# A fused attention and gated MLP kernel: the first batch's heads keep keys, queries and two value blocks in SBUF between two passes

## The chip, the core and the metric

The kernel runs on one core of one Trainium2 chip. The metric is device time in microseconds (us), the median of the runs shown. TensorE (PE) multiplies matrices, VectorE (DVE), ScalarE (ACT) and GpSimd (POOL) work element by element, SyncE (SP) issues the loads and stores. SBUF is the memory on the chip, PSUM the banks that PE writes.

## What is computed

Causal attention with a bias from a running sum, for 8 batches of 8 heads (576 tokens, head size 64), and behind it a gated MLP whose gate mixes tokens:

```python
scores = scale * np.matmul(q, k.transpose(0, 1, 3, 2))
cum = np.cumsum(np.maximum(s, 0.0), axis=-1)
bias = -(cum[:, :, :, None] - cum[:, :, None, :])
scores = np.where(causal, -1000000000.0, scores + np.minimum(bias, 0.0))
attn = softmax(scores); x = heads of attn @ v, side by side
h = gelu(x @ w_in); u, v = halves of h
v_n = (v - mean) / sqrt(var + 1e-06) * g_ln
v_s = np.einsum('ts,bsd->btd', w_sg, v_n) + b_sg[None, :, None]
out = x + (u * v_s) @ w_out
```

## The kernel before

Every batch's eight heads go through scores (PE, into PSUM), a masked reduction that also finds the maximum (DVE; CUSTOM_DVE in the profile, ISA in the order lists), exp with its sum (ACT), a reciprocal (DVE) and a scaling (POOL, ACT or DVE), PE transposes ("turned" below, with `ident`), copies from PSUM (`pT`), and the product with the values, two heads at a time. The MLP of a batch (`ffn`) has v units (values and layer norm), u units, s units (the gate, first product `ws` x `vn`) and o units (`wo`); matrices are split into a hi and a lo part (`split`), so that three products in fp32r stand for one in fp32. All matmuls of the MLP and of heads 8 to 63 work on such parts.

The first batch is special, since nothing has been split when the kernel starts. Its eight heads (`SPL = 8`) use unsplit fp32 and go through in two passes: `scores_a`/`context_a` for the first 320 tokens (`CA`), `scores_b`/`context_b` for the other 256 (`CB`) against all keys. In the first pass the bias comes from a product of `sel` with the running sums (`cc`, tile xs), in the second from two rows of running sums (`cum`) that a small load puts below the keys. Meanwhile the weights arrive as 64-bit floats (`pair<-in_w_in`), are put together on ACT and DVE (`psm<-pair`, `gt<-pair`) and split into `wi` and `wo`; `w_sg` is split into `ws` by `w_sg_part`. Before the two-pass work is through, FFN units have little to multiply; 49 matmuls on a constant (`WARM = 9`, `FILL = 40`, `psm<-wt`) fill PE's time.

The places of the first batch: `load_a` (line 702 on) brings queries and keys of the first pass into `kqs[0..2]` (heads 0 to 2, over the rings k1, q1, k2), or into `arena` (heads 3 to 7, over `wo`). `load_va` brings value blocks for the first pass into `early`, over `ws`. `load_b` brings the 256 queries and all 576 keys of the second pass anew (832 columns) into `kqs[3]`, `kqs[4]` (over vn) or into `arena` where a head of the first pass was; `load_vb` brings five value blocks anew. Upper halves of these tiles are set to 0 or 1 by memsets. Scores have three buffers while the first eight heads run: p_66, p_68 and e_71 (`pslot`), so heads 0, 3, 6 share one, as do 1, 4, 7 and 2, 5.

The order on all engines is written by a planner (`Plan`). Every step is put at a time by `POS`, the planner lists operations with their dependences and walks them by priority; `SHIFT`, a table of one offset for each operation, moves priorities. `pick` chooses the engine of a step from the letters in `ENG` and `ALT` (s ACT, g POOL, v DVE). The planner's order is fixed when the kernel is built; on the chip every engine works through its own list in order. `w_sg_part` may begin when head 5's second pass is turned (its assert), since `ws` lies over `early`.

## Time and profile before

| | |
|---|---|
| median of 3 runs | 738.69 us (736.52 to 740.17) |
| the profiled execution | 737.75 us, span 736.0 us |
| busy: PE, DVE, ACT, POOL | 726.3, 483.4, 482.8, 526.0 us |
| granted TensorE clock over the span | 0.999 |
| DMA: moved, mean rate | 88.35 MB, 120 GB/s |

The span runs from the first instruction to the last; the profiled execution's own time has 1.75 us around it. Busy times add what an engine's instructions cover. All lines of the profile carry one line number, that of the planner's `issue` (L441; L446 in the changed kernel), so work is told apart by its tiles: `p<-pss,mask` is a score piece leaving PSUM, `wi<-gt,wi` the lo part of w_in, and so on. An entry in square brackets says how long the engine had been idle and what ended that.

### The profile page before, as it was taken

Reading aid. Unit: us, or ns where it says so; the run is one execution under the profiler, and the core shown is the slowest. Engines: PE = TensorE matmul, PEld = TensorE weight load, DVE = VectorE, ACT = ScalarE, POOL = GpSimd, SP = SyncE. Lnnn points to the kernel's source line nnn. Section 1 sums busy time; section 2 is a strip of 40 time slices with the busy share of each in tenths; the row PEclk is TensorE's granted clock in tenths of the full one; section 3 lists DMA queues with packets and bytes.
Section 4 is the critical chain, followed back from the end, with each engine's and each line's share of the span. In section 5 each row is a group of like instructions: output and inputs, shape, how many; then the busy total and the mean of one; then the engine's idle time right before and its main releaser. Section 6 shows DMA issues by size and latency. Waiting matters only on the chain.

```text
span 736.0 us, 16276 instructions
## 1 busy us (share of the span) xinstructions
PE 726.3 (99%) x5337; PEld 640.8 (87%) x5337; DVE 483.4 (66%) x1524; ACT 482.8 (66%) x1306; POOL 526.0 (71%) x941
## 2 busy tenths in 40 slices
...
GB/s 210 252 234 102 199 125 121 169 141 149 128 135 133 130 115 104 124 110 124 147 86 119 123 125 127 106 92 144 132 108 119 95 135 114 61 9 34 47 9 64
DMA packets 59272, 88.35 MB, mean 120 GB/s; under 512 B 16306, under 2 KB 33972, under 8 KB 59188
## 3 DMA queue, kind: packets, MB, share of 16 engines
...
## 4 chain that ended last, share of the span: by engine, by line
PE 91%; DVE 3%; DMA 2%; POOL 2%; ACT 1%; issue 1%; SPq 1%; ACTq 0%; DVEq 0%; POOLq 0%
PE psm L441 54%; PE psp L441 21%; PE pss L441 15%; DMA pair<-in_w_in 1%; DVE p L441 1%; SPq L441 1%; DVE psm L441 1%; POOL p L441 0%; DMA raw<-in_kq 0%; POOL wi L441 0%; POOL rt L441 0%; ACT p L441 0%; DVE gt L441 0%; DVE vt L441 0%; DVE u L441 0%
## 5 line engine op out<-in xcount | busy, mean ns | idle before, releaser
L441 POOL TENSOR_SCALAR p<-p,rs 64x64 f32<-64x64 f32 (+4 forms) x396 | 177.8, 458 | 55.9 <-DVE rs L441 37.8
L441 ACT ACTIVATE p<-p,mn 64x64 f32<-64x64 f32 (+4 forms) x310 | 172.5, 558 | 57.4 <-DVE mn L441 55.7
L441 DVE CUSTOM_DVE_ANT_0 p<-pss,mask 128x448 f32<-128x448 f32 (+4 forms) x304 | 121.0, 425 | 37.0 <-PE pss L441 27.7
L441 PE MATMUL psm<-gt,wo 128*128 128x288 f32 x720 | 125.0, 299 | 0.0
L441 PE MATMUL pss<-k,q 128*128 128x288 f32 (+9 forms) x672 | 122.2, 297 | 0.2
L441 PE MATMUL psm<-xs,wi 128*128 128x288 f32 x720 | 119.3, 300 | 0.0
L441 PE MATMUL psm<-ws,vn 128*128 128x288 f32 x708 | 114.1, 297 | 0.0
L441 PEld LDWEIGHTS pss<-k,q 66*128 66x128 f32 (+3 forms) x672 | 102.2, 180 | 9.3 <-DVE mn L441 0.5
L441 POOL TENSOR_TENSOR k<-raw,k 128x576 fp32r<-128x576 f32 x54 | 77.3, 1431 | 44.8 <-ACT k L441 41.1
L441 PE MATMUL psm<-wi,xs 128*128 128x512 f32 (+1 forms) x380 | 106.6, 401 | 1.0 <-DVE gt L441 1.0
L441 PEld LDWEIGHTS psm<-gt,wo 128*128 128x128 f32 x720 | 105.3, 188 | 1.7
L441 PEld LDWEIGHTS psm<-xs,wi 128*128 128x128 f32 x720 | 102.6, 188 | 2.4 <-issue 0.4
L441 PEld LDWEIGHTS psm<-ws,vn 128*128 128x128 f32 x708 | 100.2, 188 | 0.9 <-DVE vt L441 0.3
L441 PE MATMUL psp<-pT,vf 128*64 128x64 f32 (+3 forms) x752 | 90.1, 387 | 0.0
L441 PEld LDWEIGHTS psp<-pT,vf 128*64 128x64 f32 x752 | 46.9, 137 | 43.9 <-issue 32.1
L441 PEld LDWEIGHTS psm<-wi,xs 128*128 128x128 f32 (+1 forms) x380 | 66.3, 184 | 13.2 <-DVE gt L441 1.2
L441 ACT COPY pT<-psp 128x512 f32<-128x512 f32 x130 | 72.0, 581 | 8.7 <-PE psp L441 8.1
L441 PE MATMUL psp<-ident,p 128*128 128x128 f32 x744 | 72.3, 247 | 0.3 <-POOL p L441 0.3
L441 PEld LDWEIGHTS psp<-ident,p 128*128 128x128 f32 x744 | 69.7, 140 | 3.0 <-POOL p L441 0.5
L441 DVE SCALAR_TENSOR_TENSOR u<-u,psm 128x288 f32<-128x288 f32 x120 | 52.7, 445 | 18.6 <-ACT u L441 18.2
L441 POOL TENSOR_TENSOR gt<-u,gt 128x288 fp32r<-128x288 f32 (+1 forms) x62 | 49.6, 804 | 18.7 <-ACT gt L441 18.2
L441 ACT ACTIVATION_READ_ACCUMULATOR p<-p,mn 128x1 f32 (+1 forms) x310 | 58.5, 189 | 0.0
...
## 6 DMA issues: line engine op xcount, KB each, us to landing
q<-k SPq DMA_DIRECT2D x168, 144.0 KB
...
```

The costliest lines, as they stand in the source:

```text
L441: fn(*args, **kw)
```

## The change

The eight heads of the first batch get a place each (`own`) that holds first- and second-pass data side by side: heads 0 to 2 in `kqs[0..2]`, 3 to 5 in `arena`, 1152 columns each (`TW`: 320 queries, 320 keys, then 256 keys, 256 queries); heads 6 and 7 get 1024 columns each in `kqs[3]`, where the second-pass queries take the place of the first-pass ones. `load_a` writes the first 640 columns. `load_b` loads only the 256 new keys and 256 new queries (one load of 512 columns, or two of 256 for heads 6 and 7), and the rows of running sums. `load_vb` loads three value blocks; blocks 0 and 1 are read in the second pass from where `load_va` put them (`sums_of`). So `early` is needed until the last pair of the second pass, and `w_sg_part` now begins after all four pairs (assert, and `POS["ws"]` from 7.0 to 8.2). `kqs[4]` goes. Memsets change with the places. `norm`'s first step can be put on another engine (`ra`), but its letter is ACT's as before. `SHIFT` (table cut here) and `ALT` are new throughout.

```diff
-A0 = 3
-AG = ((0,), (1,), (2,), (3, 4), (5, 6, 7))
+AG = ((0,), (1,), (2,), (3, 4), (5,), (6, 7))
+TW = 2 * S
 VG = ((0, 1), (2, 3), (4, 5, 6, 7))
 U2 = 7
-ENG = dict(kh="s", kl="g", xh="g", xl="g", gh="s", gl="g", wh="s", wl="g", wsh="s", wsl="gggv", n="g", vl="g", ev="s",
+ENG = dict(ra="s", kh="s", kl="g", xh="g", xl="g", gh="s", gl="g", wh="s", wl="g", wsh="s", wsl="gggv", n="g", vl="g", ev="s",
            ev1="v", xv="s", xz="v", xw="v", th="s", rt="g", na="sgg", nb="g", ea="ss", eb="s", eb1="vv", xa="sgss", xal="g",
            xva="s", xvb="v")
 ALT = {
...
-    "wh": "sssvvggssggg",
...
-    "nb": "gggsvsggggssvggsggv",
-    "eb1": "ssvsvsvv",
...
+    "wh": "ssssgsssgssg",
...
+    "nb": "vggsgsggsgssggsgssggsggs",
+    "eb1": "vvvvvvvv",
...
-           wu=(2.267, 6.052), ws=(7.001, 10.088), wo=(8.179, 8.76), f0=10.787, a=(0.058, 0.283), la=-0.795, va=-0.44,
+           wu=(2.267, 6.052), ws=(8.2, 10.7), wo=(8.179, 8.76), f0=10.787, a=(0.058, 0.283), la=-0.795, va=-0.44,
...
             p0, f0 = divmod(ap.offset, pat[0][0])
             f1 = f0 + sum(st * (c - 1) for st, c in pat[1:]) + 1
             out = []
+            w = (slot[1] - slot[0]) // 4
             for i, x in enumerate(slot):
-                lo, hi = max(f0, i * S), min(f1, i * S + S)
+                lo, hi = max(f0, i * w), min(f1, i * w + w)
                 if lo < hi:
-                    out.append((x, p0, p0 + pat[0][1], lo - i * S, hi - i * S))
+                    out.append((x, p0, p0 + pat[0][1], lo - i * w, hi - i * w))
             return out
         assert name in self.live.get(slot, (name,)), name
         ps = pat[0][0] or 1
...
                 prio = self.backward(lat, [t + o.busy for t, o in zip(self.start, ops)])
         if SHIFT:
             shift = np.frombuffer(zlib.decompress(base64.b85decode(SHIFT)), np.int16)
-            res = self.forward(lat, [p + 200.0 * float(x) for p, x in zip(prio, shift)])
+            res = self.forward(lat, [p + 100.0 * float(x) for p, x in zip(prio, shift)])
         return res
 
     def walk(self, left, follow, place, prio, begin=0.0, hold=False):
...
         d["raw"] = att.tile([P, S], F32, name="raw", tag="raw", bufs=1)
         nc.sync.dma_start(out=d["raw"], in_=kq[h, 0:2 * D])
 
+    def own(h):
+        return (kqs[h], 0, TW) if h < 3 else (arena, (h - 3) * TW, TW) if h < 6 else (kqs[3], (h - 6) * 1024, 1024)
+
     def load_a(i):
         g = AG[i]
-        if g[0] < A0:
-            t = kqs[g[0]][:, 0:2 * CA]
+        t, o, w = own(g[0])
+        for j, h in enumerate(g):
+            heads.setdefault((h, 0), {}).update(q=t[:, o + w * j:o + w * j + CA], k=t[:, o + w * j + CA:o + w * j + 2 * CA])
+        dst, src = t[0:D, o:o + w * len(g)], ka[:, g[0] * 2 * CA:(g[-1] + 1) * 2 * CA]
+        if len(g) > 1:
+            dst = dst.rearrange("p (h w) -> p h w", w=w)[:, :, 0:2 * CA]
+            src = src.rearrange("p (h w) -> p h w", w=2 * CA)
         else:
-            t = arena[:, (g[0] - A0) * 2 * CA:(g[-1] + 1 - A0) * 2 * CA]
-        for j, h in enumerate(g):
-            o = 2 * CA * j
-            heads[h, 0] = {"q": t[:, o:o + CA], "k": t[:, o + CA:o + 2 * CA]}
-        nc.sync.dma_start(out=t[0:D], in_=ka[:, g[0] * 2 * CA:(g[-1] + 1) * 2 * CA])
+            dst = dst[:, 0:2 * CA]
+        nc.sync.dma_start(out=dst, in_=src)
 
     def load_va(i):
         g = VG[i]
         t = early[0][:, 3 * S + g[0] * 4 * D:3 * S + (g[-1] + 1) * 4 * D]
         nc.sync.dma_start(out=t, in_=va[:, g[0] * 4 * D:(g[-1] + 1) * 4 * D])
         for j, h in enumerate(g):
-            heads[h, 0]["v"] = t[:, j * 4 * D:(j + 1) * 4 * D].rearrange("p (a d) -> p a d", d=D)
+            heads.setdefault((h, 0), {})["v"] = t[:, j * 4 * D:(j + 1) * 4 * D].rearrange("p (a d) -> p a d", d=D)
 
     def load_b(h):
+        assert (scores_a, h) in done
         d = heads[h, 1] = {}
-        w = CB + S
-        n = (3, 4, "t", 0, 1, 2, 3, 4)[h]
-        if h > 5:
-            assert (scores_b, h - 6) in done
-        if h > 1 and h < 6:
-            t = arena[:, AW:AW + w] if n == "t" else arena[:, n * w:n * w + w]
-            if n != "t":
-                assert all((scores_a, i) in done for i in range(A0, SPL))
-                nc.gpsimd.memset(t[D:P, 0:CB], 1.0)
+        t, o, _ = own(h)
+        m = o + 2 * CA
+        d["k"] = t[:, o + CA:o + CA + S]
+        if h < 6:
+            d["q"] = t[:, m + CB:m + 2 * CB]
+            nc.sync.dma_start(out=t[0:D, m:m + 2 * CB], in_=kb[h])
         else:
-            t = kqs[n][:, CA - CB:CA + S]
-        d["q"], d["k"] = t[:, 0:CB], t[:, CB:w]
-        nc.sync.dma_start(out=t[0:D], in_=kb[h])
-        nc.sync.dma_start(out=t[D:66, CB:w], in_=cum[:, h, :])
+            d["q"] = t[:, o:o + CB]
+            nc.sync.dma_start(out=t[0:D, m:m + CB], in_=kb[h][:, 0:CB])
+            nc.sync.dma_start(out=t[0:D, o:o + CB], in_=kb[h][:, CB:2 * CB])
+        nc.sync.dma_start(out=t[D:66, o + CA:o + CA + S], in_=cum[:, h, :])
 
     def load_vb(h):
         d = heads[h, 1]
-        d["v"] = att.tile([P, 5, D], F32, name="vf", tag="vf")
-        nc.sync.dma_start(out=d["v"], in_=vp[h, :, 0:5])
+        d["v"] = att.tile([P, 3, D], F32, name="vf", tag="vf")
+        nc.sync.dma_start(out=d["v"], in_=vp[h, :, 2:5])
 
     def load_v(h):
         d = heads.setdefault(h, {})
...
         nc.tensor.matmul(wm, wt.broadcast_to([P, P]), wt.broadcast_to([P, 512]), start=True, stop=True)
     nc.after = 850.0
     wo = const.tile([P, NC, 2, DM], F32R, name="wo")
-    AW = (SPL - A0) * 2 * CA
     arena = nc0.alloc_sbuf_tensor_at(f"arena_{next(Ring.serial)}", [P, NC * 2 * DM], F32, offset=Ring.top - NC * 2 * DM * 4).ap()
     nc.home[arena.tensor.name] = nc.home[wo.tensor.name]
     nc.live[nc.home[wo.tensor.name]].add(arena.tensor.name)
-    nc.vector.memset(arena[D:P, 0:2 * 2 * CA], 0.0)
-    nc.gpsimd.memset(arena[D:P, 2 * 2 * CA:AW], 0.0)
-    nc.gpsimd.memset(arena[D:P, AW:AW + CB], 1.0)
-    nc.gpsimd.memset(arena[D:P, AW + CB:AW + CB + S], 0.0)
     kqs = []
-    for i in range(5):
+    for i in range(4):
         if i < 3:
             r = pools[("k1", "q1", "k2")[i]]
-            t = nc0.alloc_sbuf_tensor_at(f"kq_{i}", [P, CA + S], F32, offset=r.at[0]).ap()
-            slots = nc.home[t.tensor.name] = tuple(r.at[0:2])
-            for x in slots:
-                nc.live[x] = {t.tensor.name}
+            t = nc0.alloc_sbuf_tensor_at(f"kq_{i}", [P, TW], F32, offset=r.at[0]).ap()
+            slots = tuple(r.at[0:2])
         else:
-            t = pools["vn"]([P, CA + S], F32, "kq", i - 1)
-        nc.gpsimd.memset(t[D:P, 0:CA], 1.0)
-        nc.gpsimd.memset(t[D:P, CA:2 * CA if i < 3 else CA + S], 0.0)
+            t = nc0.alloc_sbuf_tensor_at(f"kq_{i}", [P, 2048], F32, offset=pools["vn"].at[2]).ap()
+            slots = tuple(pools["vn"].at[2:4])
+        nc.home[t.tensor.name] = slots
+        for x in slots:
+            nc.live[x] = {t.tensor.name}
         kqs.append(t)
+
+    def plain(e, t, a, b):
+        e.memset(t[D:P, a:b], 0.0)
+
+    for i in range(3):
+        plain(nc.gpsimd, kqs[i], 0, 2 * CA)
+    plain(nc.vector, arena, 0, 2 * CA)
+    plain(nc.gpsimd, arena, TW, TW + 2 * CA)
+    plain(nc.gpsimd, arena, 2 * TW, 2 * TW + 2 * CA)
+    for i in range(2):
+        nc.gpsimd.memset(kqs[3][D:P, 1024 * i:1024 * i + CA], 1.0)
+        plain(nc.gpsimd, kqs[3], 1024 * i + CA, 1024 * i + CA + S)
+    for i in range(3):
+        for t, o in ((kqs[i], 0), (arena, i * TW)):
+            nc.gpsimd.memset(t[D:P, o + 2 * CA + CB:o + TW], 1.0)
+            plain(nc.gpsimd, t, o + 2 * CA, o + 2 * CA + CB)
     cf = moe.tile([P, S], F32, name="cf", tag="xs", bufs=4)
     nc.scalar.activation(out=st[0:BH], in_=st[0:BH], func=AF.Relu, scale=8.0)
     nc.vector.tensor_tensor_scan(out=cf[0:BH], data0=wt.bitcast(F32)[0:BH].broadcast_to([BH, S]), data1=st[0:BH],
...
                 yield 1
 
     def w_sg_part():
-        assert all((context_b, h) in done for h in range(SPL) if pslot(h) == 2)
+        assert all((xsplit, c) in done for c in range(NC))
         for j in range(NT):
             for f in range(2):
                 fs = slice(f * CH, f * CH + CH)
...
             yield 1
 
     def w_out_part():
-        assert all((scores_b, h) in done for h in range(2, 6))
+        assert all((scores_b, h) in done for h in range(3, 6))
         for c in range(NC):
             part(wide, w_out[c * P:(c + 1) * P], wo[:, c, 0, :], wo[:, c, 1, :])
             yield 1
...
 
     def norm(h, its, rs):
         c = slice(min(its), max(its) + 1)
-        nc.scalar.activation(out=rs[:, c], in_=sums[pslot(h)][:, c], func=AF.Copy, bias=1e-9)
+        e = pick("ra")
+        if e is nc.scalar:
+            e.activation(out=rs[:, c], in_=sums[pslot(h)][:, c], func=AF.Copy, bias=1e-9)
+        else:
+            e.tensor_scalar(out=rs[:, c], in0=sums[pslot(h)][:, c], scalar1=1e-9, scalar2=None, op0=ALU.add)
         nc.vector.reciprocal(out=rs[:, c], in_=rs[:, c])
         for it in its:
             r, w = ITR[it], ITW[it]
...
         with nc.group():
             for o0, o1, jt, c0, kw in parts:
                 for side, i in enumerate(pair):
-                    nc.tensor.matmul(x[D * side:D * side + D, o0:o1], heads[i, half]["v"][:, jt, :],
+                    v = heads[i, 0]["v"][:, jt, :] if jt < 2 or not half else heads[i, 1]["v"][:, jt - 2, :]
+                    nc.tensor.matmul(x[D * side:D * side + D, o0:o1], v,
                                      pts[i % NPT][:, c + c0:c + c0 + o1 - o0], **{"start": False, "stop": False, **kw})
 
     def context_a(h):
...
     va = np.concatenate([v[0:SPL, 0:CA], z, z, v[0:SPL, 0:D]], axis=1)
     return {
         "ka": np.concatenate([qt[:, :, 0:CA], kt[:, :, 0:CA]], axis=2).transpose(1, 0, 2).reshape(D, SPL * 2 * CA),
-        "kb": np.concatenate([qt[:, :, CA:S], kt], axis=2),
+        "kb": np.concatenate([kt[:, :, CA:S], qt[:, :, CA:S]], axis=2),
         "va": va.reshape(SPL, 4, P, D).transpose(2, 0, 1, 3).reshape(P, SPL * 4 * D),
         "kq": kq,
         "vp": v6.reshape(BH, 6, P, D).transpose(0, 2, 1, 3),
```

SP's list from its start, before (kq_80 to kq_82 are heads 0 to 2, pair is w_in, e_71 the value blocks, kq_83 and kq_84 the later `kqs`):

```order
L441 DMA xs_76<-in_s_t 64x576
L441 DMA kq_80<-in_ka 64x640
L441 DMA kq_82<-in_ka 64x640
L441 DMA pair_105<-in_w_in 128x1024
L441 DMA kq_81<-in_ka 64x640
L441 DMA e_71<-in_va 128x512
L441 DMA pair_121<-in_w_in 128x1024
L441 DMA arena_79<-in_ka 64x1280
L441 DMA pair_112<-in_w_in 128x1024
L441 DMA e_71<-in_va 128x512
L441 DMA kq_83<-in_kb 64x832
L441 DMA arena_79<-in_ka 64x1920
```

and after the change:

```order
L446 DMA xs_76<-in_s_t 64x576
L446 DMA pair_104<-in_w_in 128x1024
L446 DMA kq_80<-in_ka 64x640
L446 DMA pair_111<-in_w_in 128x1024
L446 DMA arena_79<-in_ka 64x640
L446 DMA kq_81<-in_ka 64x640
L446 DMA kq_82<-in_ka 64x640
L446 DMA kq_83<-in_ka 64x2x640
L446 DMA arena_79<-in_ka 64x2x640
L446 DMA e_71<-in_va 128x512
L446 DMA pair_120<-in_w_in 128x1024
```

A w_in tile has moved ahead of the first head, and all first-half loads ahead of the value blocks, the third w_in tile and the second-half loads.

POOL's list around the scalings of head 2 (e_71), before:

```order
L441 TENSOR_TENSOR wi_99<-gt_113,wi_99 128x512
L441 MEMSET e_71 128x64
L441 TENSOR_SCALAR e_71<-e_71,rs_110 64x64
L441 TENSOR_SCALAR e_71<-e_71,rs_110 128x320
L441 TENSOR_SCALAR e_71<-e_71,rs_110 64x64
L441 TENSOR_TENSOR wi_99<-gt_106,wi_99 128x512
L441 TENSOR_SCALAR xs_125<-xr_115 128x320
L441 MEMSET arena_79 64x256
```

and after:

```order
L446 TENSOR_TENSOR wi_98<-gt_105,wi_98 128x512
L446 MEMSET kq_82 64x256 x2
L446 MEMSET kq_80 64x256
L446 MEMSET e_71 128x64
L446 MEMSET kq_83 64x576
L446 TENSOR_SCALAR p_68<-p_68,rs_107 128x128
L446 TENSOR_SCALAR p_68<-p_68,rs_107 128x320
L446 MEMSET kq_80 64x256
L446 MEMSET kq_83 64x320
L446 MEMSET kq_83 64x576
L446 TENSOR_SCALAR e_71<-e_71,rs_109 128x320
L446 TENSOR_SCALAR e_71<-e_71,rs_109 64x64 x2
```

The lo part of a w_in tile that stood just ahead of head 2 is now ahead of head 1 too, and the memsets have come between.

POOL's list where the lo parts of w_sg begin, before (p_66 with rs_187 is head 6's second pass):

```order
L441 TENSOR_SCALAR p_66<-p_66,rs_187 128x512
L441 TENSOR_SCALAR p_66<-p_66,rs_187 64x64
L441 TENSOR_TENSOR xs_131<-xr_120,xs_131 128x256
L441 TENSOR_TENSOR ws_70<-u_113_185,ws_70 128x288
L441 TENSOR_TENSOR ws_70<-u_121_193,ws_70 128x288
```

and after (p_66 with rs_202 is head 8):

```order
L446 TENSOR_SCALAR p_66<-p_66,rs_202 128x448
L446 TENSOR_TENSOR ws_70<-u_125_198,ws_70 128x288
L446 TENSOR_SCALAR p_66<-p_66,rs_202 64x64
L446 TENSOR_TENSOR ws_70<-u_132_205,ws_70 128x288
L446 TENSOR_TENSOR k_151_224<-raw_219,k_150_223 128x576
L446 TENSOR_TENSOR ws_70<-u_137_210,ws_70 128x288
L446 TENSOR_TENSOR xs_138<-xr_134,xs_138 128x256
L446 TENSOR_TENSOR wo_78<-gt_200,wo_78 128x512
```

They have moved from behind head 6's second pass to behind most of head 8's scalings.

## Rows read from the trace of the kernel before

**Rows 1.** The page, busy time, share of the span and instructions of two engines.

```profile
PE 726.3 (99%) x5337; PEld 640.8 (87%) x5337; DVE 483.4 (66%) x1524; ACT 482.8 (66%) x1306; POOL 526.0 (71%) x941
```

**Rows 2.** Busy time in four stretches: us, PE, PEld, DVE, ACT, POOL, PEclk, DMA share, GB/s.

```profile
10.00:30.00 20.00, 19.26 (x141) 16.34 (x141) 14.88 (x62) 16.26 (x61) 10.08 (x22) 1.00 1.04 262
30.00:90.00 60.00, 57.37 (x418) 45.07 (x415) 57.17 (x168) 54.15 (x148) 44.60 (x71) 1.00 0.68 179
90.00:106.00 16.00, 15.69 (x107) 12.33 (x106) 13.73 (x44) 12.95 (x38) 14.35 (x32) 1.00 0.51 124
106.00:720.00 614.00, 613.86 (x4561) 548.65 (x4562) 387.24 (x1227) 394.41 (x1054) 445.56 (x791) 1.00 0.41 109
```

**Rows 3.** DMA issues of the first 60 us: out<-in, count, KB each.

```profile
vf<-in_vp SPq DMA_DIRECT2D x6, 160.0 KB
...
kq<-in_kb SPq DMA_DIRECT2D x4, 208.0 KB
arena<-in_kb SPq DMA_DIRECT2D x4, 208.0 KB
...
kq<-in_ka SPq DMA_DIRECT2D x3, 160.0 KB
```

**Rows 4.** The chain that ended last and PE's timeline, 5 to 10 us.

```profile
5.39 10.55 DMA pair<-in_w_in
...
5.26 1.03 PE L441 MATMUL pss<-kq 128*128 128x320 f32 x4
...
8.94 1.10 PE L441 MATMUL pss<-kq 128*128 128x320 f32 x4 [1.78 <-DMA kq<-in_ka]
9.75 0.56 PE L441 MATMUL pss<-xs,sel 128*128 128x192 f32 x2
```

**Rows 5.** Timelines of POOL, PE and DVE, 14 to 27 us (start, us, engine, work).

```profile
14.66 0.37 POOL L441 TENSOR_SCALAR p<-p,rs 128x128 f32<-128x128 f32 x1 [5.24 <-DVE rs L441]
...
20.14 1.27 POOL L441 TENSOR_TENSOR wi<-gt,wi 128x512 fp32r<-128x512 f32 x1 [0.93 <-ACT rs L441]
...
24.68 0.31 POOL L441 MEMSET arena<- 64x256 f32 x1
...
25.06 0.51 PE L441 MATMUL psp<-ident,e 128*128 128x128 f32 x4 [0.50 <-POOL arena L441]
...
26.02 0.36 DVE L441 CUSTOM_DVE_ANT_0 e<-pss,mask 128x192 f32<-128x192 f32 x1
```

**Rows 6.** DVE's timeline, 14 to 25 us: the entries ahead of which it waited.

```profile
16.68 0.70 DVE L441 TENSOR_SCALAR psm<-psm 128x512 int32<-128x512 int32 x1 [1.28 <-ACT psm L441]
...
19.52 0.36 DVE L441 CUSTOM_DVE_ANT_0 p<-pss,mask 128x192 f32<-128x192 f32 x1 [0.68 <-PE psp L441]
...
22.96 0.49 DVE L441 COPY xr<-psp 128x320 f32<-128x320 f32 x1 [1.61 <-PE psp L441]
...
24.11 0.17 DVE L441 RECIPROCAL rs<-rs 128x3 f32<-128x3 f32 x1 [0.65 <-ACT rs L441]
```

**Rows 7.** DVE's groups by shape, 30 to 100 us: count, busy us, mean ns.

```profile
L441 DVE SCALAR_TENSOR_TENSOR gt<-pair,psm 128x512 int32<-128x512 int32 x9 | 6.1, 674 | 0.0
L441 DVE COPY pT<-psp 128x512 f32<-128x512 f32 x7 | 4.7, 674 | 0.0
```

**Rows 8.** The tile ws: duration in ns min/median/max, first and last start.

```profile
L441 POOL TENSOR_TENSOR ws<-u,ws x6: 805/808/814, 74.4 to 87.0; 128x288 fp32r<-128x288 f32 x6
```

**Rows 9.** Timelines of PE and POOL, 57 to 104 us.

```profile
57.03 1.02 PE L441 MATMUL pss<-arena 128*128 128x448 f32 x2 [1.62 <-DVE mn L441]
...
81.18 2.29 PE L441 MATMUL psp<-pT,vf 128*64 128x256 f32 x20
...
82.92 0.81 POOL L441 TENSOR_TENSOR ws<-u,ws 128x288 fp32r<-128x288 f32 x1 [0.43 <-ACT ws L441]
...
85.21 2.36 PE L441 MATMUL psm<-wi,xs 128*128 128x512 f32 x9 [1.01 <-DVE gt L441]
...
103.22 0.80 PE L441 MATMUL psm<-ws,vn 128*128 128x288 f32 x4
```

238 lines of the change are left out of this document (121 added, 117 removed).

## The prediction, made before the changed kernel ran

> **What bounds the kernel now.** I read the page first. TensorE (PE) is busy for 99% of the span, DVE for 66% [rows 1], so a change pays only where PE has holes, or waits that the busy share hides. The table by stretches shows where [rows 2]: from 106 to 720 us PE is busy 613.86 of 614 us at a granted clock of 1.00 (the 2.4 GHz level); in the first 106 us it has the holes, and there it also runs the 49 matmuls on a constant (WARM and FILL in the code) that only fill time. So the stretch ahead of 106 us decides, and whatever is won there should reach the end one for one, because the change leaves PE's instructions equal in number and shape (4866 matmuls in the order lists of both, the same 49 fillers among them).
>
> Within that stretch two things bound in turn. From 10 to 30 us the DMA engines are full (share 1.04, 262 GB/s) while DVE is busy 14.88 of 20 us; from 30 to 90 us DVE is busy 57.17 of 60 us and the DMA share is 0.68 [rows 2]. First the loads and the latency of a head, then DVE. Each microsecond of DVE work brought forward from the second part into DVE's holes of the first is a microsecond won. The hole from 10 to 30 us is 5.12 us.
>
> **The loads.** They leave one queue in order and land in order. The second head's load came at 8.94 us, when PE waited for it, and the third w_in tile at 15.94 (5.39 + 10.55, in the chain) [rows 4]. By the sizes [rows 3], those not shown by the shapes in the order list at four bytes each, 1136 KB were due by the first and 2736 KB by the second: 1600 KB in 7.00 us, 229 KB/us.
> - Before, the load of heads 5 to 7 ends at 3680 KB: 15.94 + 944/229 = 20.1 us. After, all first-half loads stand within the first 2448 KB: 8.94 + 1312/229 = 14.7 us. The last input is 5.4 us earlier. Heads 3 and 4 are now the last to land and not heads 5 to 7; they stood at 2224 KB, 13.7 us, and lose 1.0 us, which their score buffers hide: those are free only once heads 0 and 1 are turned.
> - The price: the first head's load stands behind a w_in tile, at 816 KB: 8.94 − 320/229 = 7.5 us. Before, that head's first products ran at 5.26, but its products with the cumulative sums only at 9.75, behind the second head's load [rows 4]; without them nothing leaves PSUM. That hides the delay, so I cost it at nothing; with that cover gone it is 7.5 − 5.3 = 2.2 us.
> - The third w_in tile moves from 2736 to 3216 KB, 2.1 us later; the fourth stays (6000 KB before, 6100 after). DVE has other heads' pieces meanwhile.
> - The second half loses bytes: eight 208 KB and eight 160 KB loads [rows 3] become six of 128, four of 64 and eight of 96 KB, 2944 to 1792 KB, 5.0 us of the queue. This shows only if something waits for it. The first rows of cumulative sums, which the second half needs, stand behind 7410 KB instead of 7740, 1.4 us by 229 KB/us, so the second half can't start later than before because of them. Costed at nothing itself: it covers the earlier start.
>
> On the pieces the Trainium skill speaks against this change: its page "DMA: Bandwidth & Descriptors", section "Rules for kernel authors", wants small transfers joined, because under 64 KB one pays mostly overhead, and its section "Bandwidth" gives 0.95 us for 64 KB. By it (an estimate from that page) the four 64 KB pieces would hold the queue 3.8 us, not the 1.1 us of 256/229, and the sum would lose up to 2.7 us, so the time would be 738.0. No row of this kernel shows a 64 KB load in isolation.
>
> **The order on POOL.** Head 2's scalings stood behind the lo part of a w_in tile (POOL at 20.14, 1.27 us); the next tile, a split of xs and the memset of 24.68 came before PE could turn head 2, at 25.06, after PE had waited 0.50 us [rows 5]. Head 5 uses the same buffer as head 2: its scores could leave PSUM only at 26.02 [rows 5]. After the change the three scalings of head 2 stand ahead of every w_in tile but the first. That takes at least the 1.27 us, at most the 4.9 us from 20.14 to 25.06 off this chain; it is one of three buffers, so I count it in DVE's holes and not again.
>
> **The memsets** of the upper halves grow from few wide to more narrow ones on POOL, and half of the one on DVE leaves. POOL waits 5.24 us before its first scaling at 14.66 [rows 5]; they lie in that hole. Nothing. If the hole were gone, the eight additional 256-wide ones cost 0.31 each by the 24.68 row, 2.5 us.
>
> **The sum.** DVE's waits from 10 to 30 us that are named are 1.28 for a w_in tile through ACT, 0.68 and 1.61 for PE, 0.65 for ACT: 4.22 us [rows 6]. In each DVE had no other head's piece to go on with; with all inputs landed by 14.7 us and head 2 turned earlier I expect it to have one. Ends: 0, if the latency of three buffers alone sets them; all 5.12 plus 0.67 [rows 7], the last DVE step of the first w_in tile, which now stands ahead of the first scores and not behind them, 5.8. I take the 4.2, the waits with a name. Against it, DVE's own list ahead of the first gate product grows from 294 to 303 entries: three more copies of turned blocks at 0.674 us are 2.0 us [rows 7], and two casts of wi, two of xs and some wide scalings leave it. Ends 0 and 2.0; I take 0.8. Sum: −4.2 + 0.8 = −3.4 us. The profiled execution took 737.75 us (span 736.0), so 734.35 for it; the median of the three runs is 738.69, 0.94 above, so **735.3 us** is the forecast.
>
> **What is late next**: the moved split of w_sg. It stood in the buffer that now keeps the two value blocks until the last pair of the second pass has been summed, which PE did from 81.18 to 83.47 [rows 9]. Before, six of its lo parts ran on POOL at 0.808 us each between 74.4 and 87.0 [rows 8]. Five of the six began before that pair was summed, the fifth at 82.92 [rows 9]. Now all stand behind it: in POOL's list the first follows six of head 8's seven scalings, and the k split of head 11, head 9's scalings and a w_out part follow it. PE's first use is at 103.22 [rows 9], 15 us after the last lo part: that is the cover, and in the forecast it holds.
>
> **The rivals.**
> - *The saving in loads is hidden* (the change is made, but what it removes bounded nothing). DVE is full from 30 to 90 us and its list doesn't get shorter; if the three buffers set the first 30 us, nothing is won: 738.7, up to +0.8 for the longer DVE list. For it: DVE's waits name PE and ACT, none names a DMA [rows 6]. Against: the chain that ended last holds 10.55 us of a load [rows 4], and the DMA share is 1.04 [rows 2]. The small-piece rule would land here too.
> - *More goes than the first 30 us.* PE's waits at 57.03 (1.62 us, for DVE) and 85.21 (1.01, for DVE) [rows 9] come from the same full DVE list; if the lead also clears them, 735.3 − 2.6 = 732.7.
> - *POOL becomes the bound from 83 to 103 us.* Place: the five lo parts of w_sg that began before the last pair was summed and now can't. Price: 5 × 0.808 = 4.0 us moved into a stretch in which POOL is already busy 14.35 of 16 us [rows 2]; POOL runs in order, so head 9's scalings and the k splits behind them are late and PE runs out of other work. With no lead and the longer DVE list that is 738.7 + 4.0 + 0.8 = 743.5. It decides once POOL reaches the first gated part before PE has finished that pair, or once the last lo part is later than the first gate product in PE's list. For it: POOL's scalings of p wait in the same list. Against: the 15 us of cover, and POOL gets some scalings less (ACT takes them).
>
> **How the numbers follow.** Forecast 0.45, more than that 0.17, hidden 0.18, POOL slower 0.20. About 0.5% (3.7 us) is what a measurement of this kernel can tell from no change: 735.0 and 742.4 are the limits. The forecast's own range is 733 to 737.5; a little over half of it lies below 735.0 where the DVE list costs less than 0.8: 0.25. With 0.17 of the larger gain faster is 0.42. Slower takes the POOL case but for 0.02 where a small lead remains: 0.18. Same is the rest, 0.40. Range for 8 in 10: from 731 (738.7 less the 5.8 us and less two thirds of PE's 2.6) to 742.5, which leaves out about 0.16 above, most of the POOL case, and 0.04 below.
>
> **What would show it.** The table by stretches: DVE's holes from 10 to 30 us shrink from 5.1 to about 1 us, the DMA share there stays near 1. Head 5's first score piece leaves PSUM near 22 and not 26 us. PE's first gate product comes at about 100 us, not 103.2, and PE is full from there on. The forecast is wrong if DVE's holes only move to 30 to 60 us, if PE shows waits for ws or for heads 9 to 12, or if PE needs longer than 614 us for the same work behind the first stage.

## The result, and the profile after

| | before | changed |
|---|---|---|
| median (range, runs) | 737.84 us (736.52 to 740.17, 4) | 742.66 us (742.26 to 743.61, 4) |
| the profiled execution, its span | 737.75, 736.0 us | 742.61, 740.8 us |
| granted TensorE clock over the span | 0.999 | 0.998 |

The ratio is 1.0064, with an interval of [1.0034, 1.0093]: slower by 4.8 us, 0.16 us above the predicted range. (Ratios here are those of the comparison with its interval, not exactly the quotient of two medians.)

The page of the changed kernel, busy times, against [rows 1]: DVE does 11.3 us more, POOL 8.2 us less.

```profile
PE 727.5 (98%) x5337; PEld 642.1 (87%) x5337; DVE 494.7 (67%) x1533; ACT 485.8 (66%) x1316; POOL 517.8 (70%) x927
```

The table by stretches (us, PE, PEld, DVE, ACT, POOL, PEclk, DMA share, GB/s), first 0 to 10 us and the four of [rows 2], then 84 to 90 us:

```profile
0.00:10.00 10.00, 7.90 (x30) 6.38 (x30) 6.66 (x16) 3.40 (x5) 6.39 (x19) 1.00 0.69 186
10.00:30.00 20.00, 18.00 (x135) 15.84 (x135) 12.84 (x61) 17.12 (x65) 10.90 (x29) 1.00 0.96 247
30.00:90.00 60.00, 57.12 (x407) 44.29 (x404) 56.90 (x155) 52.74 (x140) 47.72 (x73) 0.97 0.60 162
90.00:106.00 16.00, 14.42 (x96) 11.26 (x95) 15.90 (x47) 13.09 (x39) 11.84 (x22) 1.00 0.49 131
106.00:720.00 614.00, 612.62 (x4557) 547.17 (x4554) 396.33 (x1244) 397.31 (x1065) 437.13 (x783) 1.00 0.41 110
...
84.00:86.00 2.00, 0.17 (x3) 0.13 (x2) 2.00 (x6) 2.00 (x8) 1.91 (x5) 1.00 1.02 315
86.00:88.00 2.00, 2.00 (x14) 1.90 (x15) 2.00 (x1) 2.00 (x6) 2.00 (x3) 0.52 1.05 285
88.00:90.00 2.00, 2.00 (x7) 1.60 (x6) 2.00 (x1) 1.68 (x5) 2.00 (x3) 0.63 0.53 114
```

DVE's holes from 10 to 30 us grew from 5.12 to 7.16 us, where the forecast wanted 1. From 86 to 90 us DVE is busy 4 of 4 us with one instruction, and the granted clock is 0.52 and 0.63, near the 1.2 GHz level. Wide stretches hide when time is lost, so I worked out a lag from the traces: each real matmul (fillers left out) counts with the lower quartile of the intervals behind matmuls of its kind in the kernel before; the lag at a time is how much later than the kernel before a kernel has done the same sum. Minus is a lead. It comes from one execution each: kernels that are alike up to a time agree there to some tenths (e7 and e13 until 82 us), but e3a, whose one more instruction of 0.45 us costs nothing in the median, ends 1.9 us late in its profiled execution. The other rows belong to the experiments.

| lag in us, at | 10 | 30 | 35 | 82 | 92 | 98 | 130 | 300 | 730 |
|---|---|---|---|---|---|---|---|---|---|
| changed kernel | +2.4 | −1.1 | +0.7 | −0.3 | +4.0 | +3.6 | +3.4 | +4.7 | +4.6 |
| e1 | +2.2 | −1.9 | −0.1 | −1.2 | +1.2 | +0.6 | +0.2 | +1.0 | +0.8 |
| e2 | +2.7 | −1.3 | +0.4 | 0.0 | +0.8 | +1.0 | +0.8 | +1.7 | +1.9 |
| e7 | +0.4 | −3.3 | −1.6 | −2.3 | −0.1 | −0.8 | −1.0 | +0.3 | +0.4 |
| e16 | +0.6 | −2.9 | −1.1 | −1.7 | +3.9 | +3.9 | +3.6 | +4.1 | +4.0 |
| e13 | +0.8 | −3.2 | −1.4 | −2.4 | −2.0 | −0.7 | −0.9 | +0.3 | +0.2 |
| e18 | +1.0 | −2.6 | −0.9 | −1.0 | +0.2 | +0.9 | +1.2 | +1.6 | +1.8 |
| e17 (on the kernel before) | +0.8 | +0.7 | +0.7 | +6.2 | +6.4 | +5.7 | +4.9 | +4.9 | +4.9 |

The changed kernel starts 2.4 us late, regains 3.5 us by 30 us, is even at 82 us, loses 4.4 us from 82 to 92 us and about one more near 266 us. PE's timeline shows the places (start, us, work, idle time before it and what ended it):

```profile
6.77 1.10 PE L446 MATMUL pss<-kq 128*128 128x320 f32 x4 [1.19 <-DMA kq<-in_ka]
...
11.79 1.10 PE L446 MATMUL pss<-kq 128*128 128x320 f32 x4 [1.66 <-DMA kq<-in_ka]
...
85.87 1.68 PE L446 MATMUL psp<-ident,p 128*128 128x128 f32 x12 [1.83 <-POOL p L446]
87.35 3.77 PE L446 MATMUL psm<-wi,xs 128*128 128x512 f32 x11
...
108.44 1.35 PE L446 MATMUL psm<-ws,vn 128*128 128x288 f32 x9
...
266.40 0.54 PE L446 MATMUL pss<-k,q 66*128 66x448 f32 x3 [0.81 <-DMA k<-cum]
```

The second head comes at 11.79 us, against 8.94 before [rows 4]; PE waits 1.83 us for a scaling of POOL at 85.87; the gate begins at 108.44, against 103.22 [rows 9]. DVE's timeline:

```profile
25.34 0.49 DVE L446 CUSTOM_DVE_ANT_0 e<-pss,mask 128x320 f32<-128x320 f32 x1 [1.50 <-PE psp L446]
...
85.84 5.15 DVE L446 TENSOR_TENSOR ws<-u,ws 128x288 fp32r<-128x288 f32 x1
90.91 0.45 DVE L446 CUSTOM_DVE_ANT_0 p<-pss,mask 128x288 f32<-128x288 f32 x1
...
99.62 0.41 DVE L446 TENSOR_TENSOR ws<-u,ws 128x288 fp32r<-128x288 f32 x1
```

The entry of 85.84 is the fourth lo part of w_sg. Its twin at 99.62 takes 0.41 us, this one 5.15, and head 9's score piece, for which PE's scores wait, stands behind it. POOL's timeline over the same time:

```profile
81.77 2.99 POOL L446 TENSOR_SCALAR p<-p,rs 64x64 f32<-64x64 f32 x6 [1.03 <-DVE rs L446]
84.73 0.80 POOL L446 TENSOR_TENSOR ws<-u,ws 128x288 fp32r<-128x288 f32 x1
85.50 0.31 POOL L446 TENSOR_SCALAR p<-p,rs 64x64 f32<-64x64 f32 x1
85.79 0.80 POOL L446 TENSOR_TENSOR ws<-u,ws 128x288 fp32r<-128x288 f32 x1
86.56 1.41 POOL L446 TENSOR_TENSOR k<-raw,k 128x576 fp32r<-128x576 f32 x1
87.93 0.80 POOL L446 TENSOR_TENSOR ws<-u,ws 128x288 fp32r<-128x288 f32 x1
88.70 0.72 POOL L446 TENSOR_TENSOR xs<-xr,xs 128x256 fp32r<-128x256 f32 x1
89.39 1.29 POOL L446 TENSOR_TENSOR wo<-gt,wo 128x512 fp32r<-128x512 f32 x1
```

From 84.73 POOL runs without a pause. Its row ends at 89.39 + 1.29 = 90.68, DVE's instruction at 90.99, 0.31 later: DVE waited for the instruction that was under way and was passed over by the four behind it. And the scaling that PE waits for (85.50) stands behind a lo part of w_sg.

### The profile page after: what moved, and what is told of

It reads as the page before. It is cut to its first block, busy times and chain, and to the rows that moved or that the text cites. A ratio compares the mean times of both kernels' runs of the same rounds, so it can differ in the third digit from the quotient of the medians.

```text
span 740.8 us, 16268 instructions
## 1 busy us (share of the span) xinstructions
PE 727.5 (98%) x5337; PEld 642.1 (87%) x5337; DVE 494.7 (67%) x1533; ACT 485.8 (66%) x1316; POOL 517.8 (70%) x927
## 4 chain that ended last, share of the span: by engine, by line
PE 84%; DVE 5%; DMA 4%; ACT 3%; POOL 2%; issue 1%; SPq 1%; POOLq 0%; ACTq 0%; DVEq 0%
PE psm L446 50%; PE psp L446 19%; PE pss L446 14%; DVE p L446 1%; DMA kq<-in_ka 1%; ACT p L446 1%; DMA pair<-in_w_in 1%; DVE psm L446 1%; DVE ws L446 1%; SPq L446 1%; DMA out_t<-u 1%; DMA u<-in_w_sgt 1%; POOL rt L446 0%; DMA pair<-in_w_out 0%; POOL p L446 0%
## 5 line engine op out<-in xcount | busy, mean ns | idle before, releaser
L446 POOL TENSOR_SCALAR p<-p,rs 64x64 f32<-64x64 f32 (+4 forms) x387 | 175.6, 463 | 51.9 <-DVE rs L446 35.4
L446 ACT ACTIVATE p<-p,mn 128x448 f32<-128x448 f32 (+4 forms) x310 | 172.4, 558 | 53.0 <-DVE mn L446 51.4
L446 DVE CUSTOM_DVE_ANT_0 p<-pss,mask 128x448 f32<-128x448 f32 (+4 forms) x304 | 122.5, 425 | 38.0 <-PE pss L446 32.0
L446 PE MATMUL pss<-k,q 66*128 66x288 f32 (+9 forms) x672 | 121.7, 297 | 1.4 <-DMA k<-cum 0.8
L446 PE MATMUL psm<-gt,wo 128*128 128x288 f32 x720 | 121.1, 298 | 0.0
L446 PE MATMUL psp<-pT,vf 128*64 128x512 f32 (+2 forms) x720 | 86.1, 387 | 0.0
L446 ACT COPY pT<-psp 128x512 f32<-128x512 f32 x127 | 70.4, 581 | 18.1 <-PE psp L446 17.2
L446 POOL TENSOR_TENSOR gt<-u,gt 128x288 fp32r<-128x288 f32 (+1 forms) x60 | 48.0, 806 | 47.4 <-ACT gt L446 45.6
L446 PEld LDWEIGHTS psp<-pT,vf 128*64 128x64 f32 x720 | 44.4, 137 | 42.0 <-issue 30.5
L446 ACT CAST gt<-u 128x288 fp32r<-128x288 f32 (+1 forms) x62 | 26.5, 430 | 52.3 <-DVE u L446 42.7
```

Of the source, the lines that this page charges most:

```text
L446: fn(*args, **kw)
```

## The experiments

The theory: the loss from 82 to 92 us is that one DVE instruction and the clock behind it, and the late second head takes most of what the first 30 us win. The rivals: POOL's load in that stretch (the prediction's last rival), DVE's longer list, and the load of the first half alone. All edits keep the planner's written order and change single steps: `to` gives a step to another engine, `move(k, ref)` puts it ahead of another, with `True` behind it; `wsl, 3` is the lo part in question. The kernel before, run beside each group of versions, had medians from 737.57 to 738.45 us; so versions of different groups are compared to about 1 us, best by their ratios.

**Where the 4 us from 82 to 92 us go: e1, e2, e8, e10.**

```diff
 e1 (on the changed kernel)
+    to(at["wsl", 3], "POOL")
 e2 (on e1: as many lo parts on DVE as in the changed kernel)
+    to(at["wsl", 5], "DVE")
 e8 (on the changed kernel: one place earlier in DVE's list)
+    move(at["wsl", 3], 687)
 e10 (on e2: the scaling PE waited for goes ahead of the first lo part)
+    move(667, at["wsl", 0])
```

> The one lo part of w_sg that DVE took from 85.84 to 90.99 us (5.15 us, 0.41 at 99.62 for the same shape) is done by POOL at the same place of the written order; nothing else moves. Theory 'DVE starved': DVE's subtraction stood still until POOL's run of gapless SBUF operations ended at 90.68 us. Then nothing in DVE's list from 80 to 91 us lasts over 1 us, POOL's run grows by 0.80 us, the first gate product comes near 104 and not 108.4, and the time is 742.7 - 4.7 = 738.0 (737.3 to 739.0; ratio to the kernel before 0.999 to 1.002). Rival 'POOL is the bound' (a rival of the prediction, the w_sg parts now behind the last second-pass pair): POOL gets 0.8 us more, so 742.7 to 743.5. Rival 'late w_in and late heads' (PE's own waits): no change, 742.7.

> As the run before, and in exchange DVE takes another lo part of w_sg, which POOL did from 93.47 us after an idle 2.80 us; both engines have as many of them as in the changed kernel, only another one is DVE's. Theory 'DVE starved': the place and not the count costs; DVE's op of the same shape takes 0.41 to 1.0 us, time 738.0 (737.0 to 739.0). Rival 'POOL is the bound': same load on POOL, 742.7. Rival 'DVE's list is too long': same load on DVE, 742.7.

> The changed kernel with nothing but the slow DVE operation one entry earlier in DVE's list: it then starts at about 85.25 us, inside POOL's first subtraction of the row (84.73 to 85.53), and not between the one-input scaling (85.50 to 85.81) and the row of five subtractions. In the two runs without the rest of the kernel DVE got in behind the running subtraction each time. Theory 'an arrival beside a one-input scaling that is followed by a row without a gap is passed over until the row ends': now it lasts 0.6 to 0.7 us, and the time is that of the run with the part on POOL, 739.9 (ratio to the kernel before 1.002). Rival 'any row of this length holds it': 5 us again, 742.7. Rival 'DVE's list': as many entries, 742.7.

> The swap of the two lo parts as before, and on POOL the scaling for which TensorE waited 1.85 us at 85.94 in front of the first lo part of w_sg and not behind it. Rival of the prediction 'w_sg parts late on POOL delay what stands behind them': this is its one visible place; the wait falls by 0.77 us to 1.1, time 739.0 (ratio to the swap alone 0.999), and 738.5 if the clock's fall after the wait goes too. If TensorE is not what is late there: 739.8 as with the swap alone.

Measured: e1 739.93 us, ratio 1.0019 [0.9998, 1.0040]; e2 739.79, 1.0019 [1.0000, 1.0038]; e8 740.03, 1.0028 [1.0007, 1.0048]; e10 739.68, 1.0017 [1.0000, 1.0035]. Three edits that only take the lo part away from its place (e1, e2, e8) win 2.6 to 2.9 us of median, not the 4.7 that the theory expected. In e2 both engines have the same work as in the changed kernel, and e8 moves one instruction by one place, so neither POOL's load nor DVE's list is what cost here. In e8 DVE's timeline shows the price without the row:

```profile
84.44 0.57 DVE L446 TENSOR_TENSOR ws<-u,ws 128x288 fp32r<-128x288 f32 x1
```

PE's wait for POOL stays in e2, and e10, which shortens it to 1.19 us, wins nothing: a wait of 0.82 us for a split of xs, put behind, takes its place. PE's timeline of e2:

```profile
85.94 1.22 PE L446 MATMUL psp<-ident,p 128*128 128x128 f32 x12 [1.85 <-POOL p L446]
86.99 2.79 PE L446 MATMUL psm<-wi,xs 128*128 128x512 f32 x11
```

The same wait, and yet the eleven products take 2.79 us here at a granted clock of 1.00, and 3.77 us in the changed kernel at 0.52. The clock fell in the profiled executions of e1 and e8 too (0.50 from 86 to 88 us, behind waits of 1.84 and 2.04 us); e1 loses 2.4 us from 82 to 92 us even so, the changed kernel 4.4. So the lo part costs beside the clock.

**What makes 0.45 us into 5.15: e3a, e3b, e4, e5, e9, e11.** First one more instruction of this kind in the kernel before, beside idle POOL (e3a) and in a row of POOL's (e3b).

```diff
+    g = g_b[:, 0:CH]
 e3a
+    nc.ops[643].calls.insert(0, (nc0.vector.tensor_tensor, (), dict(out=g, in0=g, in1=g, op=ALU.max)))
 e3b
+    nc.ops[604].calls.insert(0, (nc0.vector.tensor_tensor, (), dict(out=g, in0=g, in1=g, op=ALU.max)))
```

> The kernel before with one more DVE operation, SBUF to SBUF, two inputs, 128x288 (the maximum of a constant tile with itself, result unchanged), in front of the entry at 69.63 us, where POOL is idle from 68.4 to 72.6. All theories: 0.41 to 0.45 us long, time of the kernel before, plus 0 to 0.5 us.

> The same additional operation 18 entries later in DVE's list, in front of the entry at 74.80 us, where POOL runs from 73.70 without a gap: two-input subtractions until 75.98, a memset of 0.14, two more until 77.55, then one-input scalings, subtraction and copy until 80.31. Theory 'DVE starved while POOL runs two-input operations': it ends with the train, so it lasts 1.2 us if the memset lets it in, 2.8 us if only the scalings do, 5.5 us if any POOL operation holds it off; DVE is the full engine here, so the time grows by as much less 0 to 0.4. Rival 'an operation's length is its own': 0.44 us, time as in the run with the operation in POOL's idle time.

Measured: e3a 737.31 us, 0.9995 [0.9974, 1.0017], the instruction 0.445 us. e3b 740.97 us, 1.0033 [1.0007, 1.0059]; but in its profiled execution, one of its quickest (739.14), the instruction took 0.73 us, none of the three prices expected. Why its median is that high stays open. Being beside POOL is not enough; what else it takes, four kernels of nothing but such instructions had to show. They compute nothing of the reference.

```diff
 e4: DVE's subtraction once, beside rows of POOL's of one kind (here eight subtractions)
+            phase([dtt], [ptt] * 8)
 e5: DVE arrives at 13 moments of a row of different subtractions without a pause
+            phase(lead, [(1, 288), (2, 576), (3, 288), (4, 256), (1, 512), (2, 288), (0, 288)])
 e9: the row begins with a scaling (64x64, 128x512, two wide ones, or a subtraction and 64x64), or is six wide scalings
+            phase(lead, [(pts, 1, 64, 64)] + R)
+            phase(lead, [(pts, 1, 512)] + R)
 e11: which of its properties it is: 64x64, 128x64, 64x512, 128x128, a memset of 64x64; 64x64 with a 128x512 scaling inside the row
+            phase(lead, [(pts, 1, 64)] + R)
+            phase(lead, [(pts, 1, 512, 64)] + R)
```

> This kernel computes nothing of the reference (its output is constant). Eleven stretches, each twice: POOL starts a row of operations, DVE 0.7 us later one operation on 128x288, SBUF to SBUF, on tiles of its own. Theory 'DVE starved while POOL runs two-input operations without a gap': DVE's two-input operation lasts 0.41 to 0.45 us alone, 2.5 us beside four POOL subtractions of 0.80 us (3.2 less 0.7), 5.7 us beside eight, about 0.4 beside eight memsets, beside one-input scalings 0.4 if only two-input operations hold DVE off; and with one operand in PSUM 0.45. In the stretch where POOL stands still in the middle it ends in that gap. Rival 'it gets in between two POOL operations': at most 0.44 + 0.80 = 1.25 us beside four and beside eight alike. Rival 'the stretch was that one instruction's own': 0.41 to 0.45 us everywhere.

> This kernel too computes nothing of the reference. In the run before POOL's subtractions all wrote one tile and stood 0.87 us apart for 0.80 us of work, and DVE got in after 0.73 us. Here DVE's subtraction (128x288, SBUF to SBUF) arrives at thirteen points of POOL's first operations, 0.07 us apart, beside three rows: eight that write one tile, eight that write different tiles (as in the changed kernel, where they stood 0.77 apart), and the widths of the changed kernel's row (288, 576, 288, 256, 512, 288, 288). Theory 'DVE starved by a row without a gap': 0.7 us beside the first row, and up to the row's end (4 to 6 us) beside the other two, at some or all points of arrival. Rival 'DVE always gets in behind the running operation': at most 0.45 + 1.43 us in all three. The point of arrival may decide: then the two lengths alternate with it.

> Computes nothing of the reference. As the run with the three rows, but now the rows begin with, or hold, one-input scalings: a scaling of 64x64 and six subtractions; a scaling of 128x512 and six; a subtraction, a scaling of 64x64 and six subtractions; two scalings and six subtractions; six scalings. DVE's subtraction arrives at thirteen points, 0.07 us apart. Theory 'passed over when it arrives beside a one-input scaling': at those points, and at no others, it lasts until the row's end (4 to 6 us), and in the row of scalings alone to its end too (3 to 4 us). Rival 'one operation passed over, no more': at most 0.45 + 2 x 0.80 us. Rival 'never': behind the running operation, at most 1.1 us.

> Computes nothing of the reference. What of the 64x64 scaling lets the row behind it pass DVE over: six subtractions behind a scaling of 64x64, of 128x64, of 64x512, of 128x128 and behind a memset of 64x64, and a scaling of 128x512 put into the middle of the six; DVE arrives at six points, 0.07 us apart, beside the first or second operation. Theory 'the short one' (0.31 us, so that the next operation is there before DVE is served): 4 to 5 us behind 64x64, 128x64 and perhaps 128x128 (0.37), 0.7 to 1.1 behind 64x512. Theory 'half the partitions': 4 to 5 us behind 64x64 and 64x512, not behind 128x64 and 128x128. In the last row it ends behind the scaling in the middle if any other kind of operation lets DVE in, else at the row's end.

Measured, e4: DVE's timeline, alone, beside subtractions, beside memsets, and with one operand in PSUM:

```profile
6.88 0.45 DVE L557 TENSOR_TENSOR c<-a 128x288 f32<-128x288 f32 x1
...
12.77 0.73 DVE L557 TENSOR_TENSOR c<-a 128x288 f32<-128x288 f32 x1
...
26.94 0.45 DVE L557 TENSOR_TENSOR c<-a 128x288 f32<-128x288 f32 x1
...
52.27 0.46 DVE L560 SCALAR_TENSOR_TENSOR c<-a,psy 128x288 f32<-128x288 f32 x1
```

In e5, 39 arrivals took 0.45 to 1.32 us: 33 of them waited for the instruction that POOL was running and ended 0.31 to 0.32 us behind it. My theory that a row without pauses passes DVE over fell in both. e9 brought it back with a condition. DVE's timeline, behind a 64x64 scaling and behind a 128x512 one, and under it POOL's:

```profile
41.25 4.97 DVE L573 TENSOR_TENSOR c<-a,b 128x288 fp32r<-128x288 f32 x1
...
47.14 0.85 DVE L573 TENSOR_TENSOR c<-a,b 128x288 fp32r<-128x288 f32 x1
```

```profile
41.10 0.31 POOL L563 TENSOR_SCALAR f<-d,z 64x64 f32<-64x64 f32 x1 [0.48 <-ACT d L568]
41.38 4.53 POOL L560 TENSOR_TENSOR f<-d,e 128x288 fp32r<-128x288 f32 x6
...
46.99 0.69 POOL L563 TENSOR_SCALAR f<-d,z 128x512 f32<-128x512 f32 x1 [1.09 <-ACT d L568]
47.65 4.73 POOL L560 TENSOR_TENSOR f<-d,e 128x288 fp32r<-128x288 f32 x6
```

Behind the 64x64 scaling, 12 of 13 arrivals last to the end of the row, 4.0 to 5.0 us (the 13th met a pause of 0.19 us); behind 128x512 none is over 1.08. In e9's other rows the five arrivals beside or just behind a 64x64 scaling in second place took 4.8 to 5.0 us and the eight ahead of it 0.45 to 1.0; behind two wide scalings, and beside six of them, none took over 0.92, so my theory of any one-input scaling fell. e11 says which property it is, by DVE's timeline, behind 64x64, 128x64 and 64x512:

```profile
46.42 4.44 DVE L576 TENSOR_TENSOR c<-a,b 128x288 fp32r<-128x288 f32 x1
...
52.31 1.04 DVE L576 TENSOR_TENSOR c<-a,b 128x288 fp32r<-128x288 f32 x1
...
58.16 4.82 DVE L576 TENSOR_TENSOR c<-a,b 128x288 fp32r<-128x288 f32 x1
```

Long behind 64 partitions (5 of 6 arrivals at 64x64, 6 of 6 at 64x512), never over 1.04 behind 128x64, 128x128 or the memset. So in these rows it is a scaling on 64 partitions, not a short one, and after it a row of POOL's subtractions without pauses, which in the changed kernel are the entries of 85.50 and 85.79 on (a subtraction on 64 partitions was not tried). Where a 128x512 scaling stood inside the row, DVE got in there after 2.6 to 2.9 us; POOL paused 0.08 us at that point, so whether the pause or the other kind of instruction lets it in stays open, as does the reason of the whole. Nor is the condition complete: in e17 a DVE cast (0.30 us in the changed kernel) that began beside a 128x512 scaling of POOL (127.97 us) was passed over by the subtraction behind it and took 1.58 us; in e15 a subtraction behind a 64x64 scaling (94.90 us) was let in after one instruction, ahead of one on a single partition, though POOL's rows show no pause.

**The late second head: e7, e16.**

```diff
 e7 (on e2), e16 (on the changed kernel): head 5's load and the second w_in tile go behind those of heads 1 and 2
+    move(148, 102, True)
+    move(176, 148, True)
```

> The swap of the two lo parts as before, and the load of the second w_in tile and that of head 5 moved behind the loads of heads 1 and 2 (they stood ahead of head 1's, for which TensorE waited 1.64 us at 11.57; DVE needs the tile only at 18.4 us and head 5 at 24.6). Theory 'the late second head eats the lead': TensorE's second head starts at 8.7 us, the holes of DVE at 12.96 (1.38 us) and 15.19 (0.53) go, the lag against the kernel before falls from +1.3 us at 15 us to about -1.5, that at 82 us to about -2, and the time to 737.8 (ratio to the swap alone 0.997). Rival 'latency of three buffers, then DVE full': the lag at 15 us falls, that at 82 us stays within 0.5 us of the swap's, 739.5 to 740.0.

> The changed kernel with the loads of the second w_in tile and of head 5 behind those of heads 1 and 2, and nothing else; the slow DVE operation stays where it is. Theory 'two causes that add': the lag at 82 us falls by 2.0 to 2.3 us, the operation still lasts 4 to 5 us, because its place against POOL's row is the same, and the time is 742.7 - 1.1 = 741.6 (740.5 to 742.0). Rival 'the late loads were the whole cause, the slow operation only filled a wait': 738.7, as with the loads and the swap.

Measured: e7 738.66 us, 0.9996 [0.9979, 1.0013], 1.1 us under e2 and 1.0 under e10, which ran in the same group; e16 741.36, 1.0057 [1.0036, 1.0079], 1.3 us under the changed kernel. Each difference is at the edge of the noise (e16's four runs, 740.29 to 742.96, overlap with the changed kernel's 742.26 to 743.61); but e7, e13 and e15 (738.7 to 739.0), which have the loads in time, all lie under e1, e2, e8 and e10 (739.7 to 740.0). The lag at 10 us falls from 2.7 to 0.4, PE's timeline of e7 has no wait at the second head, and 2.3 us of lead stand at 82 us. At 92 us nearly all of it is gone (0.1), at 98 us 0.8 are left. The granted clock is 0.75 from 84 to 86 us and 0.50 from 86 to 88:

```profile
9.76 1.11 PE L446 MATMUL pss<-kq 128*128 128x320 f32 x4
...
83.65 1.21 PE L446 MATMUL psp<-ident,p 128*128 128x128 f32 x12 [1.83 <-POOL p L446]
84.70 4.34 PE L446 MATMUL psm<-wi,xs 128*128 128x512 f32 x11
```

In e16 the long instruction is back, and with it the whole loss (DVE's timeline):

```profile
84.33 5.15 DVE L446 TENSOR_TENSOR ws<-u,ws 128x288 fp32r<-128x288 f32 x1
```

**All of it mended, and what then keeps the lead: e13, e15, e17, e18.** e13 has e7, e10's scaling and a split of xs moved; e15 also has both lo parts on POOL and the running sums loaded earlier. Neither gained, and e15's time is above what either of its theories expected: of e13's lead of 2.0 us at 92 us, 0.7 are left at 98 and nothing at 300. So e17 prices a longer DVE list in the kernel before, and e18 takes work off DVE's in e13.

```diff
 e13 (on e7)
+    move(667, at["wsl", 0])
+    move(at["xal", 7], 690, True)
 e15 (on e13)
-    to(at["wsl", 5], "DVE")
+    move(2483, 2489)
 e17 (on the kernel before): four of DVE's copies pT<-psp three times each
+                o.calls = o.calls * 3
 e18 (on e13): four of them to ACT
+    for n in (0, 1, 3, 5):
+        o = nc.ops[at["eb1", n]]
+        o.calls = [(nc0.scalar.copy, (), kw) for fn, a, kw in o.calls]
+        o.eng = "ACT"
```

> All mends in one: the swap of the two lo parts, the loads of the second w_in tile and of head 5 behind those of heads 1 and 2, the scaling for which TensorE waited ahead of the first lo part of w_sg, and the lo part of xs (TensorE waited 0.8 us for it once the scaling came first) right behind ScalarE's copy of it. Theory: the lag at 82 us is -2.2 as with the loads alone; TensorE's wait for the scaling is 1.0 to 1.2 us and not 1.83, and its granted clock doesn't fall behind it (it fell to 0.50 for 2 us after waits of 1.8 to 2.0 us in four of five runs, and not after 1.0 and 1.2), so the lag at 92 us is -1.5 and not -0.1; time 737.3 (736.5 to 738.3, ratio to the kernel before 0.997 to 0.999). Rival 'the full DVE list gives it back': 738.7 as with the loads alone.

> All mends, and three more: both lo parts of w_sg in question are POOL's (DVE's list is one entry shorter, and DVE no longer stands 0.9 us behind ScalarE's copies for them at 93 to 95 us), and the cumulative sums for which TensorE waited 0.61 us at 261.9 leave the queue ahead of an output store and a load of x that were not ready. Theory 'the lead of 2.0 us at 92 us is given back at waits with a name' (0.27, 0.29, 0.70 and 0.53 us until 106, 0.61 at 262): without the 0.70 and the 0.61 the time is 738.7 - 1.3 = 737.4 (736.6 to 738.2; ratio to the kernel before 0.998 to 1.000). Rival 'DVE's list from 40 to 130 us is longer and takes it back wherever it can': the 0.61 alone, 738.1 to 738.7.

> The kernel before, with DVE's four copies pT<-psp that began at 60.3, 67.4, 77.2 and 80.8 us each done three times (a copy is repeated with the same source and place; nothing is left out): eight more copies of 0.67 us, 5.4 us on DVE's list between 60 and 83 us. Theory 'DVE bounds from 30 to 90 us, and a longer list is paid one for one': DVE's holes from 60 to 106 us take up 2 to 3 of the 5.4, the rest arrives at the end: 740.5 to 742.5, ratio 1.004 to 1.007. Rival 'DVE is full because it is early, PE has other work': PE's lag at 92 us stays under 1 us, 737 to 738.5, ratio within 1.001.

> The kernel with all mended (order of the first loads, the scaling that PE waited for, the w_sg parts, the split of xs), and four of DVE's copies pT<-psp, at 46.4, 48.7, 60.6 and 69.0 us, given to ACT, as the kernel before had four of its first eight of this kind: 2.7 us off DVE's list ahead of 82 us, 2.3 us on ACT's, whose busy share from 30 to 82 us is 45 of 52 us. Theory 'the lead that is lost between 82 and 98 us is lost to DVE's list': PE keeps at least 1 us more of its lead at 98 us (lag -1.7 or lower, not -0.7), 737.5 or lower against 738.7, ratio 1.000 or lower. Rival 'ACT is as full there (22.4 of 24 us from 82 to 106 us), or the lead is lost to the latency of a head': lag at 98 us -0.7 or above, ratio 1.001 to 1.003.

Measured: e13 738.69 us, 1.0016 [1.0002, 1.0031]; e15 738.96, 1.0022 [1.0008, 1.0036]; e17 742.34, 1.0054 [1.0034, 1.0073]; e18 740.52, 1.0036 [1.0020, 1.0051]. PE's timeline of e13 has the waits at which the lead goes, and under it that of e15 the same ones, longer:

```profile
97.15 1.99 PE L446 MATMUL psm<-xs,wi 128*128 128x288 f32 x13 [0.70 <-DVE vt L446]
...
106.04 0.73 PE L446 MATMUL pss<-k,q 128*128 128x448 f32 x4 [0.53 <-DVE mn L446]
```

```profile
97.07 1.99 PE L446 MATMUL psm<-xs,wi 128*128 128x288 f32 x13 [0.95 <-DVE vt L446]
...
106.45 0.74 PE L446 MATMUL pss<-k,q 128*128 128x448 f32 x4 [1.01 <-DVE rt L446]
```

Ahead of the wait of 0.70 us DVE itself waits for POOL, here for one instruction. DVE's timeline of e13, and under it POOL's:

```profile
94.92 1.52 DVE L446 TENSOR_TENSOR ws<-u,ws 128x288 fp32r<-128x288 f32 x1 [0.44 <-ACT ws L446]
96.36 0.74 DVE L446 SCALAR_TENSOR_TENSOR vt<-psm,mv,g_b 128x512 f32<-128x512 f32 x1
...
94.69 1.43 POOL L446 TENSOR_TENSOR k<-raw,k 128x576 fp32r<-128x576 f32 x1 [0.20 <-POOL p L446]
```

The last lo part of w_sg takes 1.52 us there and not 0.41: it ends 0.32 us behind POOL's split of keys, as in e5, and `vt`, for which PE waits, stands behind it. It does so in e7 (1.55) and e15 (1.46), and in e2, without the lead, not (0.66 and 0.41). So up to 0.7 of the 1.3 us that e13 loses from 92 to 98 us may be this; no run moved that lo part.

e17 shows that more work in DVE's list at this place is paid: 5.4 us more there cost 4.0 us of time. PE's timeline has a wait for the copy itself, at a moment at which PE has nothing else:

```profile
87.70 3.10 PE L441 MATMUL psp<-pT,vf 128*64 128x256 f32 x18 [2.03 <-DVE pT L441]
```

Behind it the granted clock is 0.57 and 0.58 from 88 to 92 us, so part of the 4.0 is the clock. But e18, with 2.7 us less on DVE, is slower than e13 by 1.8 us: at 82 us its lead is 1.0 and not 2.4. The table by stretches of e13, and under it a row of e18's (columns as above):

```profile
0.00:10.00 10.00, 7.47 (x29) 6.04 (x29) 6.45 (x16) 3.18 (x4) 6.38 (x19) 1.00 0.77 203
10.00:30.00 20.00, 20.00 (x159) 17.84 (x158) 14.39 (x69) 19.28 (x73) 12.08 (x32) 1.00 0.99 278
30.00:82.00 52.00, 50.94 (x362) 38.79 (x360) 49.53 (x143) 45.09 (x118) 40.61 (x61) 1.00 0.53 145
82.00:106.00 24.00, 21.14 (x141) 17.36 (x141) 21.61 (x62) 22.36 (x66) 22.09 (x34) 1.00 0.61 166
```

```profile
30.00:82.00 52.00, 51.14 (x356) 38.88 (x356) 46.19 (x132) 45.90 (x119) 39.76 (x59) 1.00 0.51 139
```

My theory that the lead is lost to DVE's list alone fell; its rival expected no less lag at 98 us than e13's (it is +0.9), and a time a little under what came. From 82 to 106 us DVE, ACT and POOL are each busy 21.6 to 22.4 of 24 us in e13. And the rows ahead say what kind of lead it is: PE has no hole from 10 to 30 us, but DVE has done 6.45 + 14.39 = 20.8 us of work by 30 us, and in the kernel before 5.80 (its row from 0 to 10 us) + 14.88 = 20.7. The lead is one of PE's products; on the engine that is full next there is none. That the lead is given back for this reason fits these runs, beside the lo part of 1.52 us; but a version in which DVE itself is ahead was not found, so it isn't shown. No version beat the kernel before.

## Why the prediction was wrong

Two steps of it failed. The forecast put the moved split of w_sg at nothing ("that is the cover, and in the forecast it holds"), and one lo part of it on DVE lasted 5.15 us beside POOL's row: away from that place the time is 2.6 to 2.9 us lower (e1, e2, e8). And the −4.2 us, DVE's waits filled and kept to the end, did not come: the loads of the second head were late, and with them in time and the lo part away the time is that of the kernel before (e7, 0.9996), not 3.4 us less. Step by step:

- **What bounds the kernel: right.** 106 to 720 us is still full (612.62 of 614 us); of the lag of 4.6 us at the end, 3.4 stand at 130 us.
- **The loads: the step failed at the second head.** I priced the delay of the first head (7.5 us, costed at nothing; its products ran at 6.77) and not that of the second, which in the same list stands behind two w_in tiles and head 5. My own rule gives it: 816 + 512 + 160 + 160 = 1648 KB, 8.94 + (1648 − 1136)/229 = 11.2 us; measured 11.79. Undoing it lowers the median by 1.0 to 1.3 us, at the edge of the noise. The last load of the first half landed at 16.23 us (by the semaphore updates in the trace), not at 14.7, against 20.11 before.
- **The third w_in tile, costed at nothing: no run shows that this was wrong.** From 30 to 35 us the changed kernel loses 1.75 us of its lead, and so does e7; but by the semaphore updates that tile lands at 17.89 us in the changed kernel and at 15.81 in e7, where it was at 15.94 before, so the loss is neither the heads' doing nor the tile's. Part of it is only order: where the kernel before stands at 30 us it has run 42 of the 49 fillers, these two 39 at the same sum of products, and at 35 us all have run all 49. Three fillers of 0.24 us each are 0.7 us, and as much of the lead at 30 us is only fillers that still had to run. The rest stays open.
- **The sum of −4.2 us: a step failed that I had taken as given.** "Each microsecond of DVE work brought forward" was to be won, and by 30 us DVE had done less than before: 6.66 + 12.84 = 19.5 against 20.7. Its holes from 10 to 30 us grew to 7.16; with the heads in time they are still 5.61 (e13, 20 less 14.39), not 1. Head 5's first score piece came at 25.34 behind a wait of 1.50 for PE, not near 22. PE gains the 3.5 us in that stretch, and e7 leads by 3.3 at 30 us, near the −3.4 of the sum; but that is luck: it has it by earlier products and the order of the fillers, not by fuller holes of DVE, and 1.6 are left at 35 us.
- **"Whatever is won there should reach the end one for one": failed.** e13 leads by 2.4 us at 82 us and ends 0.2 behind. This is the rival "the saving is hidden" (0.18), whose 738.7 is e13's time. A longer DVE list, which I had counted as +0.8, would be paid (e17: 4.0 of 5.4 us in the kernel before). Whether it is the reason isn't shown: of the 11.3 us that DVE does more in the changed kernel, 9.1 lie between 106 and 720 us (396.33 against 387.24), where PE is full, and the stretch ahead holds the long instruction's excess of 4.7 over 0.41.
- **POOL from 83 to 103 us (0.20): right in place and sign, 743.5 forecast against 742.66, wrong in its price.** It was to be five lo parts moved into POOL's list. e2 has the same load and is 2.9 us faster; the price was the one lo part on DVE, which lasted 5.15 us and which I had not priced at all. So that 743.5 lies near the measured time is luck. The cover itself held: no wait of PE names the parts of w_sg.
- **The small pieces:** no wait names the four 64 KB loads; their own cost no run shows.
- **The numbers:** the range's end of 742.5 was set to leave out most of the POOL case, whose price was wrong, so that it is missed by only 0.16 us is luck too. The second head's 1.0 to 1.3 us, taken off the −3.4, would have brought forecast and chances nearer to no change.
